# Splits moved to VectorE, early squares to ScalarE, late products over 128 rows, and a read that alternates halves

## The chip, the cores and the metric

The kernel runs on one core of one Trainium2 chip. The metric is the device time of one execution in microseconds. The kernel before was timed three times; the median is 1171.35 us (1170.88 to 1172.41).

## The reference

Three stages follow each other. Every number is float32; the weights of the second and third stage are drawn as float64, and the kernel reads their 64-bit words.

```python
# x [8, 8, 512, 64], state [8, 8, 32, 64] (batch, head, token, width), scale = 1/8
a  = softmax(scale * x @ state^T)            # token over state rows
xread = a @ state
a2 = softmax(scale * state @ x^T)            # state row over tokens
sread = a2 @ x
x = concat([xread, sread], axis=2)           # 8 * 544 = 4352 rows of 512
h = x @ w_in;  r = maximum(h, 0);  x = (r * r) @ w_out        # 512 -> 2048 -> 512
h = x @ w2_in                                                 # 512 -> 1024
solu = h * softmax(h)
out = layernorm(solu) * g_ln @ w2_out                         # 1024 -> 512
```

## The kernel before

TensorE takes operands of a rounded 32-bit type (F32R), so a number is kept as two of them: a rounded part (`hi`) and the rest (`lo`). `split` (L106) makes both: ScalarE copies into `hi` with rounding, and another engine subtracts `hi` from the source into `lo`. `triple` (L110) then makes a product from three matmuls: hi by hi (L114), hi by lo (L115), lo by hi (L116).

The read of the state is not computed token by token. For each batch of x, state and w_in are multiplied first (`sw_part` for batches 0 to 3, `late_part` for batches 4 to 7), written to DRAM, and read back by `load_sw` in chunks of 512 columns. `split_sw` (L368) splits a chunk's two tiles (`sw`), 64 splits in all, whose subtraction runs on GpSimd through the argument `eng`. `hidden` (L535) multiplies them with the attention weights `ah`, `al` of the batch into a bank of PSUM (`ps_h`, two banks), ScalarE applies Relu, and the result `r` is squared, by ScalarE in the first 16 steps (L546), by VectorE later (L548). One step later `high` (L551) rounds the square into `gh` (a cast on VectorE, L553), `low` makes the rest `gl` (VectorE, L558), and another step later `project` multiplies both with a tile of w_out into four accumulators `acc`.

A step is one column block of 128 (f) of one batch (b). The list `items` runs batches 0 and 1 in two halves (steps 0 to 31), batches 2 to 7 (steps 32 to 127), and then the rows of `sread` (b = 8, steps 128 to 143, 256 columns wide). In the first 20 steps the words of w_in and w_out are converted to 32 bits, mostly by VectorE (`convert_parts`, L182 to L199). From step 32 to 63 each second step also holds two late products (`late_part`): state tiles transposed once (`st_t`, hi and lo) by w_in tiles that hold the hi rows of one head in partitions 0 to 63 and its lo rows in partitions 64 to 127. L340 multiplies over all 128 rows, L341 the lo part of the state over the first 64.

`attention(b)` is a list of pieces that the steps before call one after the other: transposes of x (`trans_x`, L400), scores (L413, L414), softmax by row (`rows_a`, `rows_b`) and by column, transposes of the weights (`trans_a`, L507), and `sread` (L474), which multiplies x with the column weights: 32 instructions of 64 weight columns in two bursts for each batch, each recorded as two matmuls. The two heads of a pair write partitions 0 to 63 and 64 to 127 of one bank.

After the last step the third stage runs tile by tile (`up`, `solu_norm`, `trans`, `down`).

The code is not the order of the engines. A scheduler takes the instructions in the order of the program and places each on its engine by its own estimate of when it becomes ready; each engine, and the DMA queue of SyncE (SP), then runs its list strictly in order. A change in one engine's work can so move instructions of all others.

Of the kernel before, what the change touches and what calls it, by code (L numbers as in the profile page):

```python
# [8 lines left out]
F32 = mybir.dt.float32  # L9
# [3 lines left out]
AF = mybir.ActivationFunctionType  # L13
ALU = mybir.AluOpType
# [6 lines left out]
def memory_attention_relu2_solu(  # L21
# [15 lines left out]
    nc = tc.nc  # L37
    P = 128
    B, H, S, D = x.shape
# [5 lines left out]
    NT = S // P  # L45
    NHP = H // 2
    NQ = H // 4
    NF = F1 // P
# [54 lines left out]
    ]  # L103
    sr = srp.tile([P, NHP, NSR], F32, name="sr")

    def split(hi, lo, src, eng=None):  # L106
        nc.scalar.activation(out=hi, in_=src, func=AF.Copy)  # L107
        (eng or nc.vector).tensor_tensor(out=lo, in0=src, in1=hi.bitcast(F32), op=ALU.subtract)  # L108

    def triple(ps, pairs, first, last):  # L110

        n = len(pairs)
        for i, (lh, ll, rh, rl) in enumerate(pairs):
            nc.tensor.matmul(out=ps, lhsT=lh, rhs=rh, start=first and i == 0, stop=False)  # L114
            nc.tensor.matmul(out=ps, lhsT=lh, rhs=rl, start=False, stop=False)  # L115
            nc.tensor.matmul(out=ps, lhsT=ll, rhs=rh, start=False, stop=last and i == n - 1)  # L116

    def bank(name):
        return ps_m.tile([P, 512], F32, tag="m", name=name)
# [7 lines left out]
    def sw_tile(name):  # L127
        return swp.tile([P, 2, 512], F32R, tag="sw", name=name)
# [126 lines left out]
    def state_step(a, t):  # L255

        ps = bank("ps_st")
        for bb in range(2):
            for q in range(NQ):
                o = (bb * NQ + q) * P  # L260
                nc.tensor.transpose(
                    ps[:, o : o + P], a[:, 2 * t + bb, q].rearrange("p i d -> p (i d)"), ident
                )
        v = ps.rearrange("p (b q i n) -> p q n b i", b=2, q=NQ, i=2)
        for i in range(2):
            o = bd[i][t]
            split(o[:, :, i], o[:, :, 1 - i], v[:, :, :, :, i])
# [31 lines left out]
    def late_state(step):  # L299
        nb = B // 2  # L300
        if step == 0:
            t = stgp.tile([P, H, 2, D], F32, tag="stg", name="st_l")
            for b in range(nb):
                for i in range(2):
                    nc.sync.dma_start(
                        out=t[b * NS : (b + 1) * NS, :, i, :], in_=state[nb + b].rearrange("h n d -> n h d")
                    )
            late_st["f32"] = t
        else:
            t = late_st["f32"]  # L310
            ps = bank("ps_st")
            for k in range(4):
                nc.tensor.transpose(
                    ps[:, k * P : (k + 1) * P], t[:, 4 * (step - 1) + k].rearrange("p i d -> p (i d)"), ident
                )
            o = u_tile("st_t")
            split(o[:, 0, :], o[:, 1, :], ps)
            late_st[step - 1] = o
# [11 lines left out]
    def late_part(u, i):  # L330
        c, k = divmod(u, NM)
        if i == 0:
            sw_ev[0] = evp.tile([P, 2, 512], F32, tag="ev", name="ev_sw")
        ev = sw_ev[0]
        ps = bank("ps_sw")
        t = late_w[u]
        h = 2 * k + i
        st = late_st[h // 4]
        o = (h % 4) * P
        nc.tensor.matmul(out=ps, lhsT=st[:, 0, o : o + P], rhs=t[:, i, :], start=True, stop=False)  # L340
        nc.tensor.matmul(out=ps, lhsT=st[:D, 1, o : o + P], rhs=t[:D, i, :], start=False, stop=True)  # L341
        nc.scalar.activation(out=ev[:, i, :], in_=ps, func=AF.Copy)
        if i == 1:
            nc.sync.dma_start(out=sw2_d[:, 2 * k : 2 * k + 2, c * FC : (c + 1) * FC], in_=ev)
            late_w.pop(u)
# [22 lines left out]
    def split_sw(b, c):  # L368
        st = loading.pop((b, c))
        loaded[b, c] = []  # L370
        for q in range(NQ):
            t = sw_tile("sw")
            split(t[:, 0, :], t[:, 1, :], st[:, q, :], nc.gpsimd)
            loaded[b, c].append(t)

    def load_w1in(c, kk):
# [16 lines left out]
    def attention(b):  # L393
# [82 lines left out]
        def sread(half):  # L476
            if half == 0:
                v["ps_sr"] = bank("ps_sr")
            ps = v["ps_sr"]
            for hp in (2 * half, 2 * half + 1):  # L480
                for i in range(2):
                    h = 2 * hp + i
                    for t in range(NT):
                        nc.tensor.matmul(  # L484
                            out=ps[i * D : (i + 1) * D, hp * NS : (hp + 1) * NS],
                            lhsT=xs_t[b][hp][:, t, i, :],
                            rhs=v["e2", t // 2][:, t % 2, h * NS : (h + 1) * NS],
                            start=(t == 0),
                            stop=(t == NT - 1),
                        )  # L490
            if half == 1:
                nc.scalar.activation(
                    out=sr[:, :, b * NS : (b + 1) * NS],
                    in_=ps[:, : NHP * NS].rearrange("p (h n) -> p h n", n=NS),
                    func=AF.Copy,
                )
# [13 lines left out]
        def at(f, *a):  # L510
# [14 lines left out]
            [at(cols_t, 0)],  # L525
            [at(cols_t, 1)],
            [at(sread, 0)],
            [at(sread, 1)],
        ]

# [3 lines left out]
    def hidden(blk, f, w, ah, al, n):  # L534

        c0 = (f % FPC) * P
        ps = ps_h.tile([P, 512], F32, tag="h", name="ps_h")[:, :n]
        pairs = [
            (w[k][:, 0, c0 : c0 + P], w[k][:, 1, c0 : c0 + P], ah[:, k, :], al[:, k, :])
            for k in range(ah.shape[1])  # L540
        ]
        triple(ps, pairs, True, True)
        r = rp.tile([P, 512], F32, tag="r", name="r")[:, :n]
        nc.scalar.activation(out=r, in_=ps, func=AF.Relu)  # L544
        if len(done) < NF:
            nc.scalar.activation(out=r, in_=r, func=AF.Square)  # L546
        else:
            nc.vector.tensor_tensor(out=r, in0=r, in1=r, op=ALU.mult)  # L548
        return r

    def high(b, f, n, r):  # L551
        gh = gp.tile([P, 512], F32R, tag="gh", name="gh")[:, :n]
        nc.vector.tensor_copy(out=gh, in_=r)  # L553
        return b, f, n, r, gh

    def low(b, f, n, r, gh):
# [76 lines left out]
    while first:  # L633
        for piece in first.pop(0):
            piece()
    fetch_pair(NM)
    split_sw(0, 0)
    begin("o", 0)
    for t in range(1, B // 2):
# [56 lines left out]
    def up(s, blk, t):  # L696
        xh, xl, _ = x2_t[blk]
        ps = ps_2[s % 2].tile([P, F2], F32, tag="h2", name="h2")
        for k in range(NM):
            for lt, hl in ((xh, (0, 1)), (xl, (0,))):  # L700
                for i in hl:
                    for a in range(2):
                        nc.tensor.matmul(  # L703
                            out=ps[:, a * 512 : (a + 1) * 512],
                            lhsT=lt[:, k, t * P : (t + 1) * P],
                            rhs=w2[k][:, i, a * 512 : (a + 1) * 512],
                            start=(k == 0 and lt is xh and i == 0),
                            stop=(k == NM - 1 and lt is xl),
                        )
        return ps  # L710
# [78 lines left out]
    done = []  # L789
    for s, (b, f) in enumerate(items):  # L790
# [24 lines left out]
        if b == B:  # L815
# [9 lines left out]
            if f in (12, 13):  # L825
                split_x2(0)
        h = high(*squares.pop(0)) if squares else None
        if ws == 2 and 1 <= w < B - 1:
            att = attention(w + 1)
# [9 lines left out]
        if h:  # L839
            pend.append(low(*h))  # L840
        squares.append((b, f, n, hidden(b, f, loaded[b, f // FPC], *a1_t[b], n)))
        done.append((b, f))
        if s // FPC + 1 < len(chunks) and chunks[s // FPC + 1][0] < B:
            nxt = chunks[s // FPC + 1]
            if s % FPC == 1:
                load_sw(*nxt)
            elif s % FPC == 2:
                split_sw(*nxt)
        if b < 2 and f in (NF - 4, NF - 3):
            i = f - NF + 4  # L850
# [12 lines left out]
        for m in range(4):  # L863
            if s < 24 or m == 0:
                advance()
            if sw is not None and m < 2:
                sw_part(sw, m)
            if late is not None and m > 1:
                late_part(late, m - 2)
            if job:  # L870
                project(*job, m)
# [22 lines left out]
    for s in range(1, len(tiles) + 2):  # L894
        if s == 1:
            reload_w2(7, 1)
        if s < len(tiles):
            blk, t = tiles[s]
            i = order.index(blk) + 1
# [7 lines left out]
            ps = up(s, blk, t)  # L907
# [36 lines left out]
```

## Time and profile before

| | |
|---|---|
| median of three runs | 1171.35 us |
| profiled execution | 1172.12 us, span 1170.3 us |
| granted TensorE clock, mean | 0.983 |
| TensorE busy | 1124.8 us (96%) |
| VectorE busy | 746.5 us (64%) |
| ScalarE busy | 484.1 us (41%) |
| GpSimd busy | 143.9 us (12%) |
| DMA queue of SyncE | 132.68 MB, 36.5% of 16 engines |

The span is the time from the first to the last instruction that the profile shows; the profiled execution is 1.8 us longer than its span. Busy times are unions: matmuls overlap each other, and one of 0.39 us may start 0.23 us after the one before it, so the distance between starts tells what a matmul costs, and not how long it lasts. Step 0 begins at about 57 us, step 16 at 162 us, step 32 at 243 us, step 64 at 421 us, step 128 at 712 us; the third stage fills the time from 760 us on.

### The profile page before, as it was taken

What the parts mean: (1) busy time and instruction counts of PE and PEld (TensorE: products, weight loads), DVE (VectorE), ACT (ScalarE), POOL (GpSimd) and SP (SyncE); (2) the same over time, 40 slices, a digit from 0 to 9 for tenths busy, and PEclk for the clock granted to TensorE, in tenths of its full rate; (3) what the DMA queues carried; (4) which work ended last, traced back from release to release, by engine and by line L of the source; (5) the groups of instructions that cost most, each with busy time, mean ns of one, the idle gap of its engine ahead of it and who ended that gap; (6) DMA issues with size and microseconds to landing.
All of it is one profiled execution on the core that took longest, in us unless ns stands there. A gap on an engine that the chain in (4) does not pass through costs nothing.

```text
span 1170.3 us, 15242 instructions
## 1 busy us (share of the span) xinstructions
PE 1124.8 (96%) x5672; PEld 914.3 (78%) x5672; DVE 746.5 (64%) x1357; ACT 484.1 (41%) x845; POOL 143.9 (12%) x122
## 2 busy tenths in 40 slices
PE   4787999999999999999999999999999999999997
PEld 2556778777777778888888889988888888888886
DVE  7869999778557569588585554765545454445442
ACT  4657664345445345244342212443434333334232
POOL 0101302132221122222111110000000000000000
PEclk9788999999999999999999999999999999999999
DMA  8775794567565454331310114621101011000000
GB/s 228 242 231 184 267 286 127 161 184 223 180 180 176 128 165 135 89 119 64 91 37 18 73 54 150 229 82 54 64 19 63 18 63 37 28 18 27 19 26 30
DMA packets 93323, 133.66 MB, mean 114 GB/s; under 512 B 45248, under 2 KB 45760, under 8 KB 93248
## 3 DMA queue, kind: packets, MB, share of 16 engines
q1 hardware_dynamic: 93248, 132.68, 36.5%
q8 instruction: 45, 0.74, 0.3%
q14 instruction: 30, 0.25, 0.1%
HBM read 83.37 MB, written 49.28 MB: 113 GB/s over the span
## 4 chain that ended last, share of the span: by engine, by line
PE 84%; DVE 8%; DMA 3%; ACT 2%; issue 1%; POOL 1%; SPq 0%; POOLq 0%; ACTq 0%; DVEq 0%
PE h L703 15%; PE acc L114 10%; PE acc L115 9%; PE acc L116 9%; PE ps_o L754 5%; PE ps_o L752 5%; PE ps_o L753 5%; PE ps_h L114 5%; PE ps_h L116 5%; PE ps_h L115 5%; PE ps_t L742 2%; PE ps_sr L484 2%; PE ps_sw L341 1%; DMA stg<-sw_d 1%; PE ps_x L400 1%
## 5 line engine op out<-in xcount | busy, mean ns | idle before, releaser
L114 PE MATMUL acc<-gh,w1out 128*128 128x512 f32 (+1 forms) x576 | 223.5, 389 | 5.3 <-DVE gh L553 3.9
L115 PE MATMUL acc<-gl,w1out 128*128 128x512 f32 (+1 forms) x576 | 219.4, 381 | 0.0
L116 PE MATMUL acc<-gh,w1out 128*128 128x512 f32 (+1 forms) x576 | 219.2, 381 | 0.0
L548 DVE TENSOR_TENSOR r<-r 128x512 f32<-128x512 f32 (+1 forms) x128 | 99.5, 778 | 119.4 <-ACT r L544 119.3
L108 POOL TENSOR_TENSOR sw<-stg,sw 128x512 fp32r<-128x512 f32 x64 | 101.0, 1590 | 417.1 <-ACT sw L107 245.3
L703 PE MATMUL h<-w,x2h 128*128 128x512 f32 x544 | 148.6, 395 | 0.0
L544 ACT ACTIVATE r<-ps_h 128x512 f32<-128x512 f32 (+1 forms) x144 | 82.3, 572 | 134.9 <-PE ps_h L116 131.2
L114 PEld LDWEIGHTS acc<-gh,w1out 128*128 128x128 f32 x576 | 109.4, 190 | 34.1 <-issue 7.4
L116 PEld LDWEIGHTS acc<-gh,w1out 128*128 128x128 f32 x576 | 109.3, 190 | 20.7
L115 PEld LDWEIGHTS acc<-gl,w1out 128*128 128x128 f32 x576 | 109.5, 190 | 19.8 <-issue 0.5
L703 PEld LDWEIGHTS h<-w,x2h 128*128 128x128 f32 x544 | 99.7, 188 | 18.9
L114 PE MATMUL ps_h<-ah,sw 128*128 128x512 f32 x256 | 107.7, 421 | 0.9 <-ACT ah L107 0.9
L752 PE MATMUL ps_o<-w,lh 128*128 128x512 f32 x272 | 106.1, 390 | 1.0 <-ACT lh L107 1.0
L754 PE MATMUL ps_o<-w,ll 128*128 128x512 f32 x272 | 106.2, 390 | 0.6 <-DVE ll L108 0.6
L753 PE MATMUL ps_o<-w,lh 128*128 128x512 f32 x272 | 105.9, 389 | 0.0
L116 PE MATMUL ps_h<-ah,sw 128*128 128x512 f32 x256 | 101.9, 398 | 1.4 <-POOL sw L108 1.4
L558 DVE TENSOR_TENSOR gl<-r,gh 128x512 fp32r<-128x512 f32 (+1 forms) x144 | 100.5, 698 | 3.4
L115 PE MATMUL ps_h<-al,sw 128*128 128x512 f32 x256 | 101.0, 394 | 0.0
L721 ACT ACTIVATE e<-h,nm 128x1024 f32<-128x1024 f32 x34 | 38.0, 1116 | 143.7 <-DVE nm L718 143.7
L717 DVE TENSOR_REDUCE nm<-h 128x1 f32<-128x1024 f32 x34 | 41.6, 1224 | 86.1 <-PE h L703 86.1
L553 DVE CAST gh<-r 128x512 fp32r<-128x512 f32 (+1 forms) x144 | 80.6, 560 | 9.8 <-ACT r L546 1.9
L703 PE MATMUL h<-w,x2l 128*128 128x512 f32 x272 | 83.8, 389 | 0.0
(131 smaller groups left out, 1715.9 us busy)
## 6 DMA issues: line engine op xcount, KB each, us to landing
stg<-sw_d SPq DMA_DIRECT2D x128, 128.0 KB, 3.0
sw_d<-ev_sw SPq DMA_DIRECT2D x28, 512.0 KB, 4.1
st<-in_moe_w_out_dram SPq DMA_DIRECT2D x24, 512.0 KB, 4.7
xs<-in_x_dram SPq DMA_DIRECT2D x64, 128.0 KB, 3.2
w1i_d<-w1in SPq DMA_DIRECT2D x16, 512.0 KB, 3.9
st<-in_moe_w_in_dram SPq DMA_DIRECT2D x16, 512.0 KB, 5.3
x_d<-ev_x SPq DMA_DIRECT2D x16, 512.0 KB, 2.7
w1in<-w1i_d SPq DMA_DIRECT2D x32, 256.0 KB, 4.7
```

Of the source, the lines that this page charges most:

```text
L108: (eng or nc.vector).tensor_tensor(out=lo, in0=src, in1=hi.bitcast(F32), op=ALU.subtract)
L114: nc.tensor.matmul(out=ps, lhsT=lh, rhs=rh, start=first and i == 0, stop=False)
L115: nc.tensor.matmul(out=ps, lhsT=lh, rhs=rl, start=False, stop=False)
L116: nc.tensor.matmul(out=ps, lhsT=ll, rhs=rh, start=False, stop=last and i == n - 1)
L544: nc.scalar.activation(out=r, in_=ps, func=AF.Relu)
L548: nc.vector.tensor_tensor(out=r, in0=r, in1=r, op=ALU.mult)
L553: nc.vector.tensor_copy(out=gh, in_=r)
L558: nc.vector.tensor_tensor(out=gl, in0=r, in1=gh.bitcast(F32), op=ALU.subtract)
L703: nc.tensor.matmul(out=ps[:, a * 512 : (a + 1) * 512], lhsT=lt[:, k, t * P : (t + 1) * P], rhs=w2[k][:, i, a * 512 : (a + 1) * 512], start ...
L752: nc.tensor.matmul(out=ps, lhsT=a, rhs=wt[:, 0, o : o + 512], start=(k == 0), stop=False)
L753: nc.tensor.matmul(out=ps, lhsT=a, rhs=wt[:, 1, o : o + 512], start=False, stop=False)
L754: nc.tensor.matmul(out=ps, lhsT=bb, rhs=wt[:, 0, o : o + 512], start=False, stop=(k == NK - 1))
```

## The change

Four edits. (1) `split_sw` no longer names GpSimd: its 64 subtractions go to VectorE, and `split` loses the argument. (2) For steps 0 to 31 (b < 2) ScalarE makes both the rounded square and the square, from `r`, in `high`; VectorE neither squares nor casts there. From step 32 on VectorE still squares, as `r` times the product in PSUM, and casts. (3) L341 multiplies over 128 rows, so that the lo part of the state also meets the lo part of w_in. (4) `sread` runs over the four token blocks outside and the two heads inside, so that its matmuls alternate between the two halves of the partitions.

```diff
-    def split(hi, lo, src, eng=None):
+    def split(hi, lo, src):
         nc.scalar.activation(out=hi, in_=src, func=AF.Copy)
-        (eng or nc.vector).tensor_tensor(out=lo, in0=src, in1=hi.bitcast(F32), op=ALU.subtract)
+        nc.vector.tensor_tensor(out=lo, in0=src, in1=hi.bitcast(F32), op=ALU.subtract)
...
         nc.tensor.matmul(out=ps, lhsT=st[:, 0, o : o + P], rhs=t[:, i, :], start=True, stop=False)
-        nc.tensor.matmul(out=ps, lhsT=st[:D, 1, o : o + P], rhs=t[:D, i, :], start=False, stop=True)
+        nc.tensor.matmul(out=ps, lhsT=st[:, 1, o : o + P], rhs=t[:, i, :], start=False, stop=True)
...
-            split(t[:, 0, :], t[:, 1, :], st[:, q, :], nc.gpsimd)
+            split(t[:, 0, :], t[:, 1, :], st[:, q, :])
...
             for hp in (2 * half, 2 * half + 1):
-                for i in range(2):
-                    h = 2 * hp + i
-                    for t in range(NT):
+                for t in range(NT):
+                    for i in range(2):
+                        h = 2 * hp + i
...
         nc.scalar.activation(out=r, in_=ps, func=AF.Relu)
-        if len(done) < NF:
-            nc.scalar.activation(out=r, in_=r, func=AF.Square)
-        else:
-            nc.vector.tensor_tensor(out=r, in0=r, in1=r, op=ALU.mult)
+        if len(done) >= 2 * NF:
+            nc.vector.tensor_tensor(out=r, in0=r, in1=ps, op=ALU.mult)
         return r
 
     def high(b, f, n, r):
         gh = gp.tile([P, 512], F32R, tag="gh", name="gh")[:, :n]
-        nc.vector.tensor_copy(out=gh, in_=r)
+        if b < 2:
+            nc.scalar.activation(out=gh, in_=r, func=AF.Square)
+            nc.scalar.activation(out=r, in_=r, func=AF.Square)
+        else:
+            nc.vector.tensor_copy(out=gh, in_=r)
         return b, f, n, r, gh
```

The scheduler's lists change in the first 32 steps above all. Three places follow, each before and after. Numbers behind a name tell tiles of one name apart.

SP's queue ahead of step 0 to 2, before (`st64` are words of w_in or w_out, `xs` a head of x for attention 1, `sw_d` and `w1i_d` go out to DRAM):

```order
L289 DMA sw_d0_57<-ev_sw_522 256x1x512
L213 DMA w1i_d2_64<-w1in_534 256x1x512
L289 DMA sw_d1_58<-ev_sw_581 256x1x512
L213 DMA w1i_d3_65<-w1in_593 256x1x512
L289 DMA sw_d2_59<-ev_sw_606 256x1x512
L390 DMA xs_630<-in_x_dram 128x4x64
L289 DMA sw_d3_60<-ev_sw_618 256x1x512
L390 DMA xs_633<-in_x_dram 128x4x64 x2
L390 DMA xs_636<-in_x_dram 128x4x64 x2
L390 DMA xs_639<-in_x_dram 128x4x64 x2
L137 DMA st64_645<-in_moe_w_in_dram 128x1024
L137 DMA st64_647<-in_moe_w_out_dram 128x1024
```

and after:

```order
L137 DMA st64_643<-in_moe_w_out_dram 128x1024
L287 DMA sw_d2_59<-ev_sw_475 128x512
L287 DMA sw_d3_60<-ev_sw_485 128x512
L213 DMA w1i_d0_62<-w1in_463 256x1x512
L137 DMA st64_645<-in_moe_w_in_dram 128x1024
L213 DMA w1i_d1_63<-w1in_492 256x1x512
L289 DMA sw_d0_57<-ev_sw_522 256x1x512
L213 DMA w1i_d2_64<-w1in_534 256x1x512
L289 DMA sw_d1_58<-ev_sw_581 256x1x512
L213 DMA w1i_d3_65<-w1in_593 256x1x512
L289 DMA sw_d2_59<-ev_sw_606 256x1x512
L390 DMA xs_630<-in_x_dram 128x4x64 x2
```

The load `st64_645`, tile 8 of w_in (counted from 0), moved from behind all loads of x to a place ahead of the first, behind the first `w1i_d` of its group.

VectorE's list in steps 0 to 3 up to the second score of attention 1 (`xl` and `st` belong to attention 1), before:

```order
L199 SCALAR_TENSOR_TENSOR w1out_407<-cu_686,cz_683 128x512
L188 SCALAR_TENSOR_TENSOR cu_751<-st64_643,cu_751 128x512
L553 CAST gh_773<-r_740 128x512
L558 TENSOR_TENSOR gl_790<-r_740,gh_773 128x512
L553 CAST gh_841<-r_799 128x512
L558 TENSOR_TENSOR gl_863<-r_799,gh_841 128x512
L553 CAST gh_924<-r_872 128x512
L558 TENSOR_TENSOR gl_955<-r_872,gh_924 128x512
L108 TENSOR_TENSOR xl_655<-ps_x_649,xh_654 128x512
L419 TENSOR_TENSOR st_658<-ps_s_659,st_658 64x512
L108 TENSOR_TENSOR xl_670<-ps_x_664,xh_669 128x512
L419 TENSOR_TENSOR st_658<-ps_s_702,st_658 64x512
```

and after:

```order
L192 SCALAR_TENSOR_TENSOR ch_759<-st64_643,cz_747 128x512
L188 SCALAR_TENSOR_TENSOR cu_756<-st64_645,cu_756 128x512
L192 SCALAR_TENSOR_TENSOR ch_762<-st64_645,cz_753 128x512
L198 TENSOR_SCALAR cz_747<-ch_759 128x512
L198 TENSOR_SCALAR cz_753<-ch_762 128x512
L199 SCALAR_TENSOR_TENSOR w1out_697<-cu_750,cz_747 128x512
L199 SCALAR_TENSOR_TENSOR w1in_698<-cu_756,cz_753 128x512
L560 TENSOR_TENSOR gl_790<-r_740,gh_772 128x512
L560 TENSOR_TENSOR gl_863<-r_799,gh_840 128x512
L108 TENSOR_TENSOR xl_655<-ps_x_649,xh_654 128x512
L560 TENSOR_TENSOR gl_955<-r_872,gh_923 128x512
L419 TENSOR_TENSOR st_658<-ps_s_659,st_658 64x512
```

The casts are gone, and the conversions of two tiles (`st64_643`, w_out for step 2, and `st64_645`) now stand ahead of attention 1; before, they stand behind its third `xl`.

TensorE's list in attention 1, before, from the first transposes of x to the last score (`ps_x`, `ps_s`), and the first product of step 2 (`gh_841`):

```order
L400 MATMUL ps_x_664<-ident_142,xs_633 128x128 x4
L413 MATMUL ps_s_702<-xh_669,bd1_0_150 128x512
L414 MATMUL ps_s_702<-xl_670,bd1_0_150 128x512
L400 MATMUL ps_x_707<-ident_142,xs_636 128x128 x4
L413 MATMUL ps_s_717<-xh_712,bd0_0_146 128x512
L414 MATMUL ps_s_717<-xl_713,bd0_0_146 128x512
L400 MATMUL ps_x_722<-ident_142,xs_639 128x128 x4
L413 MATMUL ps_s_775<-xh_727,bd1_0_150 128x512
L414 MATMUL ps_s_775<-xl_728,bd1_0_150 128x512
L425 MATMUL ps_r_780<-ident_142,st_658 128x128
L114 MATMUL acc0_814<-gh_841,w1out_698 128x512
L115 MATMUL acc0_814<-gl_863,w1out_698 128x512
```

and after, where `gh_840` is step 2's:

```order
L114 MATMUL acc0_813<-gh_840,w1out_697 128x512
L115 MATMUL acc0_813<-gl_863,w1out_697 128x512
L116 MATMUL acc0_813<-gh_840,w1out_697 128x512
L413 MATMUL ps_s_702<-xh_669,bd1_0_150 128x512
L114 MATMUL acc1_814<-gh_840,w1out_697 128x512
L115 MATMUL acc1_814<-gl_863,w1out_697 128x512
L414 MATMUL ps_s_702<-xl_670,bd1_0_150 128x512
L400 MATMUL ps_x_707<-ident_142,xs_636 128x128 x4
L116 MATMUL acc1_814<-gh_840,w1out_697 128x512
L114 MATMUL acc2_815<-gh_840,w1out_697 128x512
L115 MATMUL acc2_815<-gl_863,w1out_697 128x512
L116 MATMUL acc2_815<-gh_840,w1out_697 128x512
```

Step 2's products now stand between the scores of attention 1; before, they stand behind the last of them.

## Rows read from the trace of the kernel before

**Rows 1.** Busy time of each engine by stretch; first the columns.
```profile
core 0: us, PE busy (x) PEld busy (x) DVE busy (x) ACT busy (x) POOL busy (x), PEclk, DMA share, GB/s
57.00:162.00 105.00, 92.65 (x432) 71.10 (x433) 91.45 (x179) 68.27 (x124) 18.22 (x8) 0.92 0.73 241
162.00:242.70 80.70, 77.55 (x413) 63.05 (x412) 68.84 (x117) 35.59 (x65) 18.16 (x12) 1.00 0.61 163
242.70:420.60 177.90, 177.90 (x865) 133.32 (x864) 114.09 (x191) 79.68 (x139) 34.19 (x23) 1.00 0.59 177
420.60:496.30 75.70, 75.37 (x402) 62.01 (x401) 58.38 (x100) 31.46 (x56) 16.98 (x12) 1.00 0.42 127
```

**Rows 2.** Timeline of TensorE about one late product: start, us, engine, line.
```profile
302.75 0.39 PE L116 MATMUL acc<-gh,w1out 128*128 128x512 f32 x1
302.97 0.39 PE L340 MATMUL ps_sw<-w1in,st_t 128*128 128x512 f32 x1
303.29 0.50 PE L341 MATMUL ps_sw<-w1in,st_t 64*128 64x512 f32 x1
303.72 0.50 PE L114 MATMUL acc<-gh,w1out 128*128 128x512 f32 x1
304.06 0.39 PE L115 MATMUL acc<-gl,w1out 128*128 128x512 f32 x1
```

**Rows 3.** The line L341: count, duration in ns (min/median/max), first and last start.
```profile
L341 PE MATMUL ps_sw<-w1in,st_t x32: 492/498/499, 248.2 to 416.4; 64*128 64x512 f32 x32
```

**Rows 4.** Timeline of TensorE: a burst of the state's read and what follows.
```profile
321.05 1.43 PE L484 MATMUL ps_sr<-e,xs 128*64 128x32 f32 x32
322.41 0.50 PE L114 MATMUL ps_h<-ah,sw 128*128 128x512 f32 x1
```

**Rows 5.** The line L484, as in rows 3.
```profile
L484 PE MATMUL ps_sr<-e,xs x512: 222/223/244, 53.2 to 644.8; 128*64 128x32 f32 x171
```

**Rows 6.** Busy time of L484 alone in two stretches of that burst.
```profile
321.00:321.26 0.26, 0.21 (x4) 0.21 (x4) 1.00 1.07 229
321.52:321.78 0.26, 0.26 (x16) 0.26 (x12) 1.00 0.13 24
```

**Rows 7.** Groups by form: line, operation, count | busy us, mean ns | idle before.
```profile
L108 POOL TENSOR_TENSOR sw<-stg,sw 128x512 fp32r<-128x512 f32 x64 | 101.0, 1590 | 417.1 <-ACT sw L107 245.3 <-PE ps_h L116 82.9 <-DMA stg<-sw_d 58.3
L548 DVE TENSOR_TENSOR r<-r 128x512 f32<-128x512 f32 x112 | 92.8, 829 | 108.7 <-ACT r L544 108.6
L553 DVE CAST gh<-r 128x512 fp32r<-128x512 f32 x128 | 75.9, 593 | 8.7 <-ACT r L546 1.9 <-PE acc L116 1.1
L108 DVE TENSOR_TENSOR al<-ps_a,ah 128x512 fp32r<-128x512 f32 x16 | 11.0, 686 | 10.6 <-ACT ah L107 10.6
L546 ACT ACTIVATE r<-r 128x512 f32<-128x512 f32 x16 | 10.1, 630 | 0.1
```

**Rows 8.** The lines L548 and L553, as in rows 3.
```profile
L548 DVE TENSOR_TENSOR r<-r x128: 417/691/1789, 164.0 to 758.4; 128x512 f32<-128x512 f32 x112, 128x256 f32<-128x256 f32 x16
L553 DVE CAST gh<-r x144: 293/427/1552, 59.7 to 758.9; 128x512 fp32r<-128x512 f32 x128, 128x256 fp32r<-128x256 f32 x16
```

**Rows 9.** Timeline of SP's DMA issues before step 2's weights.
```profile
66.70 5.17 SPq L390 DMA_DIRECT2D xs<-in_x_dram  x6
71.92 0.62 SPq L137 DMA_DIRECT2D st<-in_moe_w_in_dram  x1
```

**Rows 10.** Timeline of VectorE in attention 1; in brackets idle time and what ended it.
```profile
77.05 0.43 DVE L182 TENSOR_SCALAR cz<-st 128x512 uint32<-128x512 uint32 x1 [0.20 <-DMA st<-in_moe_w_in_dram]
86.74 0.69 DVE L435 TENSOR_REDUCE mx<-ps_r 128x16 f32<-128x512 f32 x1 [2.22 <-PE ps_r L425]
```

**Rows 11.** Timeline of TensorE behind attention 1's scores.
```profile
81.50 0.79 PE L114 MATMUL acc<-gh,w1out 128*128 128x512 f32 x1 [1.12 <-ACT w1out L195]
86.21 0.93 PE L425 MATMUL ps_r<-ident,st 128*128 128x128 f32 x7
103.96 0.77 PE L114 MATMUL acc<-gh,w1out 128*128 128x512 f32 x1 [3.95 <-DVE gh L553]
```

## The prediction

> **What bounds the kernel now.** I read the busy time by stretch first [rows 1]. From 242.70 to 420.60 us (steps 32 to 63) TensorE is busy for all 177.90 us at full clock, and from 420.60 to 496.30 (steps 64 to 79) for 75.37 of 75.70. VectorE has 114.09 and 58.38 us of work there. So from step 32 on the time is TensorE's own: a cycle that TensorE no longer spends is a cycle off the end, and one saved on VectorE is worth nothing. Before that it is otherwise. In steps 0 to 15 (57 to 162 us) VectorE works 91.45 of 105 us, TensorE 92.65 at a mean granted clock of 0.92, and in steps 16 to 31 TensorE idles 80.70 - 77.55 = 3.15 us. There TensorE waits for others, and the order in which VectorE works decides.
>
> Then the order of time on TensorE inside the full stretch, to see what its cycles go to. A product over 128 rows and 512 columns starts 0.22 to 0.23 us after the one before it (302.75 to 302.97). The late product over 64 rows breaks this [rows 2]: it starts 0.32 us after L340, the next one 0.43 us after it, and the one after that another 0.34 us later. 302.97 to 304.06 is 1.09 us for three starts that take 0.68 elsewhere.
>
> Last, the front: what TensorE waits for between 69 and 104 us [rows 9 to 11].
>
> **The change part by part.**
>
> *Late products over 128 rows.* Each L341 costs 1.09 - 0.68 = 0.41 us beyond an ordinary product. It is no longer work: the 64-row product streams the same 512 columns, and lasts longer (498 ns) than a full one (0.39). There are 32 [rows 3], all in the stretch without idle time: 32 x 0.41 = 13.1 us. The stage confirms the size: steps 32 to 63 take 5.56 us each (177.90/32), steps 64 to 79 take 75.70/16 = 4.73, and the 0.83 between them is one late pair a step, which would be 2 x 0.23 at the ordinary rate: 0.37 too much, x 32 = 12 us. Over 128 rows L341 has the shape of L340, which costs the ordinary step wherever no L341 stands beside it. Bounds: 0 (if something else than the row count breaks the rhythm) to 13.1. I take 13.0. What is late next: VectorE, at 114 us of work in then 165, still has room.
>
> *The state's read.* A burst is 32 records in 1.43 us [rows 4], some 1.21 from first start to last start, since a record lasts 0.22 [rows 5]. In its first 0.21 us four records run, some 60 ns each. In its middle 16 records touch a window of 0.26 us [rows 6]; with 0.22 us each that is 16/0.48, one per 30 ns: there a second half's records run beside the first's. Alternating halves should give that rate from the start: 32 x 0.03 = 0.96, so 0.25 us less a burst. There are 512/32 = 16 bursts, four of them in the front where TensorE waits anyway; 12 x 0.25 = 3.0 us. Bounds: 3.0 gained, or, if every alternation is served at the first window's rate, 32 x 0.06 = 1.92, 0.71 lost a burst and 8.5 in all. I take 3.0, because the middle of the burst is the very case of two halves in flight.
>
> The Trainium skill says otherwise in one place: "TensorE: Matmul & The Clock Gate", Part 3, has weight loads overlap running products only where the row groups differ, and the two halves here differ in columns alone. By that rule alternating gains nothing, and the sum is 3 us higher. The middle of the burst, at twice the rate of its head with the rows unchanged, speaks against it. "TensorEngine Tiling (Array Packing)", Key Properties, lets different tiles load and multiply in parallel, which is what the trace shows.
>
> *Splits from GpSimd to VectorE.* 64 instructions of 1590 ns leave GpSimd [rows 7]. On VectorE a subtract of that size takes 686 ns (al, with an operand in PSUM): 64 x 0.69 = 44 us more. But GpSimd's work slows VectorE today: the square L548 takes 691 ns in the median and 1789 at most, the cast L553 427 and 1552 [rows 8], and their means are 829 and 593 [rows 7]. That is 112 x 0.138 + 128 x 0.166 = 36.7 us on these two lines alone. So VectorE's load from step 32 on stays about where it is, 64 to 77% of the stretch [rows 1], and hides the splits. Without that cover each would cost at most its 0.69.
>
> *Square and rounded part on ScalarE for steps 0 to 31.* VectorE loses 16 casts (0.43 each) in steps 0 to 15 and 16 casts and 16 squares in steps 16 to 31: 6.9 us and 16 x (0.43 + 0.69) = 17.9 us. ScalarE gains 16 and 32 squares of 630 ns [rows 7], 10 and 20 us, beside 68.27 of 105 and 35.59 of 80.70 now: it has the room. In exchange come at most 8 splits (5.5 us) and 12 (8.3 us), as many as GpSimd ran in these stretches [rows 1]. VectorE net: 1.4 us and 9.6 us less, more with the slowing gone.
>
> *What the new order does to the front.* SP issues tile 8 of w_in (st64_645, counted from 0) at 71.92, behind eight loads of x whose last six take 5.17 us [rows 9]. VectorE meets its words at 77.05 and waits for them [rows 10], and the conversion of step 2's w_out stands behind that. So the first of step 2's twelve products starts at 81.50, after a wait for w1out, and they take 4.7 us, part of it at half clock, before the scores' transposes at 86.21 [rows 11]. VectorE has waited 2.22 us for them at 86.74. After the change SP issues that tile 12 places earlier, VectorE converts both tiles ahead of attention 1, and TensorE has step 2's products between the links of the score chain, where it idles today. The 4.7 us block leaves the path. At 103.96 TensorE has waited 3.95 us for a cast on VectorE; that cast is ScalarE's now, and the gl behind it comes as early as VectorE's queue lets it. I add the 1.4 us of VectorE above and 1 us of slowing: 7.1 us for steps 0 to 15. Of the 3.15 us of idle time in steps 16 to 31, I take 2. Before step 0 two splits join a full VectorE queue, 2 x 0.69 at most, and end 0.9 us sooner each than on GpSimd: 0.7 lost, give or take. Bounds for the front together: 2 us lost (the splits, nothing gained) to 24 gained (12.35 us of idle time, 8% of 105 us of clock, and the 3.15).
>
> *The multiply that reads PSUM (step 32 on).* Same engine, same duration (686 against 691 ns). But a bank of ps_h is now free after VectorE's multiply, not after ScalarE's Relu. There are two banks: from the end of a layer's product to the next use of its bank pass two steps less two products, 2 x 4.73 - 2 x 6 x 0.23 = 6.7 us; Relu and multiply need 1.3. I count nothing; the third rival below says what happens if VectorE is over 5 us late.
>
> **Sum:** 13.0 + 3.0 + 7.1 + 2.0 - 0.7 = 24.4 us. The profiled execution took 1172.12 us, 0.77 above the median of the runs, so 1171.35 - 24.4 = 1147 us.
>
> **Rivals.**
>
> *Only TensorE's cycles come off.* Attention 1 still begins when its x lands, and VectorE, with the splits in its queue, is as late after it as today. For it: VectorE works 91 of 105 us. Against it: the block at 81.50 waits for an order, not for work. 1171.35 - 13.0 - 3.0 + 0.7 = 1156.
>
> *The front gives more.* If steps 0 to 15 end without idle time and at full clock, up to 24 us instead of 9: halfway there the time is 1139. Against it: the transfers, at 0.73 of their engines already [rows 1].
>
> *VectorE holds the banks: slower than before.* In steps 32 to 143 splits, w2 conversions and attention come in clusters; if VectorE runs over 5 us behind the Relu, TensorE waits for a bank at L114 each time. It decides from 24.4/112 = 0.22 us a step on; at 0.3 us a step the time is 1147 + 34 = 1181. For it: VectorE is at 77% in steps 64 to 79. Against it: the slowing by GpSimd goes as the splits come.
>
> *Alternating halves is served one by one.* 8.5 us lost instead of 3.0 gained: 1158.5. The case of the page's rule in its harder form.
>
> **How the numbers follow.** My forecast 0.56 (its own range 1141 to 1152), TensorE's cycles alone 0.22, more from the front 0.12, halves one by one 0.06, banks 0.04. 1138 to 1157 leaves out the upper part of the second and fourth, the far end of the third and the banks, under 0.2 together. About 0.2% (2.3 us) is what a measurement of this kernel can tell from no change. Only the banks, or several losses at once, reach it: faster 0.95, same 0.01, slower 0.04.
>
> **What would show it.** In the profile after: L340, L341 and their neighbours all at 0.23 us, and steps 32 to 63 some 165 us long; bursts of L484 under 1.0 us from first to last start; no GpSimd work beside VectorE before step 32, and L553's median as its mean; step 2's products between 69 and 81 us. I am wrong if the 64-row rhythm persists with 128 rows, if L114 into ps_h waits for VectorE, or if the stretch before step 32 is no shorter.

## The result, and the profile after

The changed kernel takes 1143.28 us (median of four runs, 1141.79 to 1144.04) against 1171.88 for the kernel before on the same chip: a ratio of 0.9755, 95% interval 0.9738 to 0.9772, 28.6 us less. The forecast was 1147, with a range from 1138 to 1157.

The profiled execution took 1141.79 us, the fastest of the four. The stretches of [rows 1] (steps 0 to 15, 16 to 31, 32 to 63, 64 to 79), with the columns of that group:

```profile
48.10:152.20 104.10, 94.73 (x512) 73.25 (x512) 92.47 (x189) 82.08 (x149) 0.00 (x0) 0.95 0.79 259
152.20:228.50 76.30, 76.22 (x411) 62.47 (x410) 51.46 (x94) 54.18 (x97) 2.58 (x2) 1.00 0.62 172
228.50:392.50 164.00, 164.00 (x865) 134.49 (x865) 110.27 (x207) 79.72 (x138) 9.40 (x7) 1.00 0.65 192
392.50:467.10 74.60, 74.60 (x401) 61.42 (x401) 55.73 (x108) 31.54 (x56) 5.18 (x4) 1.00 0.42 131
```

Steps 32 to 63 fell from 177.90 to 164.00 us, steps 64 to 79 from 75.70 to 74.60. Step 32 begins at 228.5 instead of 242.7. Steps 16 to 31 hold almost no idle time of TensorE any more (76.22 us busy of 76.30, before 77.55 of 80.70). In the whole stretch from 228.5 to 700 us the trace lists no wait of TensorE. From step 80 on the two kernels differ by 1.0 us.

TensorE about a late product, as in [rows 2]:

```profile
294.19 0.39 PE L116 MATMUL acc<-gh,w1out 128*128 128x512 f32 x1
294.42 0.39 PE L340 MATMUL ps_sw<-w1in,st_t 128*128 128x512 f32 x1
294.64 0.39 PE L341 MATMUL ps_sw<-w1in,st_t 128*128 128x512 f32 x1
294.87 0.39 PE L114 MATMUL acc<-gh,w1out 128*128 128x512 f32 x1
295.10 0.39 PE L115 MATMUL acc<-gl,w1out 128*128 128x512 f32 x1
```

Every start is 0.22 to 0.23 us behind the one before; the 0.32, 0.43 and 0.34 of [rows 2] are gone. A burst of the state's read, as in [rows 4]:

```profile
301.34 1.12 PE L484 MATMUL ps_sr<-e,xs 128*64 128x32 f32 x32
302.40 0.50 PE L114 MATMUL ps_h<-ah,sw 128*128 128x512 f32 x1
```

1.12 us instead of 1.43. With the last record's 0.22 taken off, the first and last start lie 0.90 us apart instead of 1.21.

SP's issues about tile 8 of w_in (its load is the second row), to be held against [rows 9]:

```profile
47.94 0.56 SPq L213 DMA_DIRECT2D w1i_d<-w1in  x1
48.54 1.39 SPq L137 DMA_DIRECT2D st<-in_moe_w_in_dram  x1
...
64.68 5.51 SPq L390 DMA_DIRECT2D xs<-in_x_dram  x6
```

It is issued at 48.54 us, no longer at 71.92. TensorE in attention 1, where [rows 11] have the block at 81.50:

```profile
70.74 0.63 PE L400 MATMUL ps_x<-ident,xs 128*128 128x128 f32 x4 [1.68 <-DMA xs<-in_x_dram]
71.12 0.48 PE L116 MATMUL acc<-gh,w1out 128*128 128x512 f32 x1
71.44 0.39 PE L114 MATMUL acc<-gh,w1out 128*128 128x512 f32 x1
71.67 0.40 PE L115 MATMUL acc<-gl,w1out 128*128 128x512 f32 x1
71.90 0.40 PE L116 MATMUL acc<-gh,w1out 128*128 128x512 f32 x1
72.14 0.43 PE L413 MATMUL ps_s<-xh,bd 128*128 128x512 f32 x1
```

The `acc` products fill the places between the links of the score chain. VectorE's lines, as in [rows 7]:

```profile
L546 DVE TENSOR_TENSOR r<-r,ps_h 128x512 f32<-128x512 f32 x96 | 65.8, 685 | 90.5 <-ACT r L544 90.3
L108 DVE TENSOR_TENSOR sw<-stg,sw 128x512 fp32r<-128x512 f32 x64 | 45.2, 708 | 22.9 <-ACT sw L107 22.2 <-DMA xs<-in_x_dram 0.5
L555 DVE CAST gh<-r 128x512 fp32r<-128x512 f32 x96 | 40.7, 424 | 4.2
```

The square's mean fell from 829 to 685 ns, the cast's from 593 to 424. The 64 splits cost VectorE 45.2 us, where the prediction had 44.

The longest wait of TensorE ahead of step 32 is for one `gl` (engine and line, what it waited for, us in total, times, longest):

```profile
PE acc L115 <- DVE gl L560: 2.9, 1, 2.9
```

It stands at 97.52 us, shortly ahead of step 6, as the 3.95 us wait for a cast does in the kernel before [rows 11].

### The profile page after: what moved, and what is told of

The parts are those of the page before. It is cut to its first block, busy times and chain, and to the rows that moved or that the text cites. A ratio compares the mean times of both kernels' runs of the same rounds, so it can differ in the third digit from the quotient of the medians.

```text
span 1140.1 us, 15182 instructions
## 1 busy us (share of the span) xinstructions
PE 1099.8 (96%) x5672; PEld 908.3 (80%) x5672; DVE 712.0 (62%) x1373; ACT 511.0 (45%) x893; POOL 40.8 (4%) x58
## 4 chain that ended last, share of the span: by engine, by line
PE 89%; ACT 4%; DVE 3%; DMA 3%; issue 1%; SPq 0%; POOLq 0%; POOL 0%; ACTq 0%
PE h L705 16%; PE acc L114 10%; PE acc L116 10%; PE acc L115 10%; PE ps_h L114 6%; PE ps_h L116 5%; PE ps_h L115 5%; PE ps_o L756 5%; PE ps_o L754 5%; PE ps_o L755 5%; PE ps_t L744 2%; PE ps_sr L484 1%; PE ps_x L400 1%; DMA st<-in_moe_w_out_dram 1%; PE ps_sw L340 1%
## 5 line engine op out<-in xcount | busy, mean ns | idle before, releaser
L114 PE MATMUL acc<-gh,w1out 128*128 128x512 f32 (+1 forms) x576 | 218.5, 381 | 2.8 <-ACT w1out L195 1.8
L116 PE MATMUL acc<-gh,w1out 128*128 128x512 f32 (+1 forms) x576 | 218.9, 380 | 0.0
L546 DVE TENSOR_TENSOR r<-r,ps_h 128x512 f32<-128x512 f32 (+1 forms) x112 | 72.4, 647 | 102.1 <-ACT r L544 101.9
L560 DVE TENSOR_TENSOR gl<-r,gh 128x512 fp32r<-128x512 f32 (+1 forms) x144 | 95.6, 665 | 11.9 <-ACT r L553 8.9
L731 ACT ACTIVATE j<-e,mu 128x1024 f32<-128x1024 f32 x34 | 39.1, 1151 | 54.6 <-DVE mu L728 50.6
L756 PEld LDWEIGHTS ps_o<-w,ll 128*128 128x128 f32 x272 | 51.1, 188 | 12.0 <-DVE ll L108 1.5
```

The costliest lines, as they stand in the source:

```text
L546: nc.vector.tensor_tensor(out=r, in0=r, in1=ps, op=ALU.mult)
L560: nc.vector.tensor_tensor(out=gl, in0=r, in1=gh.bitcast(F32), op=ALU.subtract)
L731: nc.scalar.activation(out=j, in_=e, func=AF.Square, bias=mu, accum_out=var)
L756: nc.tensor.matmul(out=ps, lhsT=bb, rhs=wt[:, 0, o : o + 512], start=False, stop=(k == NK - 1))
```

## The experiments

Each was timed beside the kernel before on one chip; that kernel's medians there were 1172.04, 1171.65 and 1171.55 us. The changed kernel's 1143.28 us, with which some of them are compared, is that of the section above. A reader of the profiles has to know how far two executions of one list drift apart. The three rows below are of the changed kernel, of the kernel with L341 over 64 rows, and of the one with GpSimd's splits from batch 2 on, all for 20 to 60 us (columns as in [rows 1]):

```profile
20.00:60.00 40.00, 28.87 (x173) 20.13 (x173) 35.99 (x81) 28.56 (x57) 0.00 (x0) 0.87 0.78 259
```
```profile
20.00:60.00 40.00, 29.64 (x169) 21.86 (x170) 34.14 (x77) 26.81 (x53) 0.00 (x0) 0.79 0.75 245
```
```profile
20.00:60.00 40.00, 29.72 (x166) 21.85 (x166) 33.42 (x75) 26.37 (x52) 0.00 (x0) 0.72 0.72 238
```

Their lists are the same there, yet TensorE's mean granted clock was 0.87, 0.79 and 0.72, and step 0 began at 48.1, 49.6 and 51.2 us. So for the front (everything ahead of step 32) a difference of 3 us between two profiles proves nothing, and medians decide. By its own profile the changed kernel gained 14.2 us ahead of step 32; by the medians it is 28.6 less the 16.0 that lie behind step 32, 12.6. (Of these, 0.6 belong to edit 4: two of its bursts lie just ahead of step 32.)

**Edit 3 alone, and undone.**

```diff
# on the kernel before
+        nc.tensor.matmul(out=ps, lhsT=st[:, 1, o : o + P], rhs=t[:, i, :], start=False, stop=True)
# on the changed kernel
+        nc.tensor.matmul(out=ps, lhsT=st[:D, 1, o : o + P], rhs=t[:D, i, :], start=False, stop=True)
```

Alone: 

> The kernel before with edit 3 alone (L341 over 128 rows); every engine's list of instructions is that of before. Row count breaks the rhythm: L340, L341 and the products behind them start 0.23 us apart, steps 32 to 63 shrink from 177.9 to about 165 us, the total falls by 13 us to 1158.5 (1157.5 to 1160). Rival, the late pair costs this much for another reason (its bank, its tile of w_in, the ScalarE copy behind it): 1171.5, with the starts still 0.32 and 0.43 us apart.

Measured 1159.73 us, ratio 0.9893 (0.9873 to 0.9912), 12.3 less. Undone: 

> The changed kernel with edit 3 undone (L341 over 64 rows again; the lists of all engines are those of the changed kernel). If edit 3's gain stands by itself whatever the rest does: 1143.3 + 12.3 = 1155.6, steps 32 to 63 back from 164.0 to 176 us. If it needs the earlier squares or splits: under 1150.

Measured 1156.53 us, ratio 0.9882 (0.9865 to 0.9899): 13.25 more than the changed kernel. L341 in the two kernels, alone and undone (columns as in [rows 3]):

```profile
L341 PE MATMUL ps_sw<-w1in,st_t x32: 389/389/395, 247.7 to 404.1; 128*128 128x512 f32 x32
```
```profile
L341 PE MATMUL ps_sw<-w1in,st_t x32: 493/498/498, 235.0 to 402.3; 64*128 64x512 f32 x32
```

No list moves in either, so the row count by itself sets the 498 ns and, as the times show, the cost. Steps 32 to 63 took 165.7 us alone and 176.7 undone.

**Edit 4 alone.** The diff is that of the change to `sread`.

> The kernel before with edit 4 alone (sread alternates halves). Two halves in flight: a burst's first-to-last start falls from 1.21 to 0.90 us; 12 bursts behind step 32 give 12 x 0.31 = 3.7 us, the four in the front 0 to 1.2: 1167.2 (1166 to 1168.5). Rival, the shorter bursts of the changed kernel come from something else in it: bursts stay at 1.2 us and the time at 1171.5.

Measured 1169.98 us, ratio 0.997 (0.9955 to 0.9986), nine runs from 1165.2 to 1171.3: 2.1 less, and above the range that was expected. TensorE in its trace:

```profile
322.67 1.13 PE L484 MATMUL ps_sr<-e,xs 128*64 128x32 f32 x32
323.72 0.50 PE L114 MATMUL ps_h<-ah,sw 128*128 128x512 f32 x1
```

The burst is short by the order alone. Behind step 32, where ten of the twelve bursts lie, its profile is 3.1 us shorter than that of before (1.2 in steps 32 to 63, 1.9 in steps 64 to 127). 1.6 us went back to the front, where the runs scatter.

**Edit 1 alone, edit 2 alone.**

```diff
# edit 1 on the kernel before
-            split(t[:, 0, :], t[:, 1, :], st[:, q, :], nc.gpsimd)
+            split(t[:, 0, :], t[:, 1, :], st[:, q, :])
```

> The kernel before with edit 1 alone (all 64 splits on VectorE). Theory A, the order makes the front's gain: this edit alone moves the load of w_in tile 8 ahead of the x loads and spreads step 2's twelve products over attention 1, so steps 0 to 15 end some 8 to 10 us sooner and the rest is unchanged (32 to 63 still 177.9): 1162 (1160 to 1165). Theory B, relief of VectorE by the squares and casts made the gain: here VectorE only gets 44 us more work and no relief, so 1171 to 1175. Theory C, GpSimd no longer slows VectorE: the gain is spread over steps 0 to 31 in proportion to the splits there (20 of 64), 2 to 5 us: 1168.

Measured 1164.32 us, ratio 0.9926 (0.9909 to 0.9943): 7.7 less.

> The kernel before with edit 2 alone (ScalarE squares and rounds up to step 32). Its lists keep the load of w_in tile 8 behind the x loads and step 2's twelve products in one block ahead of attention 1's transposes. Theory A (order): only steps 16 to 31 gain, 2 to 4 us, steps 0 to 15 about 1: 1168 (1166.5 to 1170). Theory B (relief of VectorE): most of the front's 14 us comes here, 1160 to 1163. Theory C (GpSimd's slowing): 1170 to 1171.5.

Measured 1169.59 us, ratio 0.9978 (0.9963 to 0.9993): 2.5 less. The relief of VectorE (theory B) falls: the edit that loads VectorE with 44 us more brought three times as much as the one that unloads it. But the 7.7 us of edit 1 are not all in steps 0 to 15: 3.1 of them are in steps 16 to 31 (77.7 us instead of 80.8), so theory A alone doesn't hold either.

**Edit 2 undone.** 

> The changed kernel with edit 2 undone (VectorE squares and rounds in the first 32 steps as before). The three other edits by themselves then: 1143.3 + 2.5 = 1146 if edit 2's gain is the same with and without the splits; up to 1149 if VectorE, which has the splits now, needs the relief.

Measured 1146.36 us, ratio 0.9786 (0.9771 to 0.9801): 3.1 more than the changed kernel, the same as edit 2 alone within the runs' scatter.

**Which part of edit 1: two splits, or the other 62.** In each of the three runs `split` has its argument `eng` back.

```diff
# the first chunk's two back on GpSimd
+            split(t[:, 0, :], t[:, 1, :], st[:, q, :], nc.gpsimd if (b, c) == (0, 0) else None)
# all but these
+            split(t[:, 0, :], t[:, 1, :], st[:, q, :], None if (b, c) == (0, 0) else nc.gpsimd)
# those of batches 2 to 7
+            split(t[:, 0, :], t[:, 1, :], st[:, q, :], nc.gpsimd if b >= 2 else None)
```

Two: 

> The changed kernel with two of the 64 splits, those of the first chunk, back on GpSimd. That alone brings back the old list around attention 1: w_in tile 8 behind the x loads, step 2's twelve products in one block ahead of the transposes. Theory A (the order makes most of the front's gain): 5 to 9 us lost before step 8, 1148 to 1152. Theory C (GpSimd slows VectorE): two splits are nothing, 1143 to 1145.

Measured 1148.70 us, ratio 0.9811 (0.979 to 0.9832): 5.4 lost by two instructions out of 64. TensorE in its trace:

```profile
80.94 0.79 PE L114 MATMUL acc<-gh,w1out 128*128 128x512 f32 x1 [1.12 <-ACT w1out L195]
...
85.80 1.01 PE L425 MATMUL ps_r<-ident,st 128*128 128x128 f32 x7
```

That is the block of [rows 11] again, with the same wait of 1.12 us ahead of it. The two splits themselves begin at 34.8 and 48.4 us, and the trace lists no wait of TensorE's matmuls for them (one weight load waits 0.8 us): the order costs the time. It costs it there. Summed over its matmuls, TensorE has started 64,000 columns by 71.1 us in this trace and 80,000 by 90.4 us. In the changed kernel's it is 71.1 and 84.3 us, in the two other traces of its lists (the rows above) 72.0 and 83.9, 74.4 and 87.7.

Sixty-two: 

> The changed kernel with 62 of the 64 splits back on GpSimd; only those of the first chunk stay on VectorE, and with them the new list around attention 1. Theory A: the gain of steps 0 to 11 stays, and what splits beside VectorE cost in steps 12 to 31 is lost, 1 to 4 us: 1144.5 to 1147.5. Theory C: nearly all of the 7 us that edit 1 gained in the front alone is lost, 1149 to 1151.

Measured 1149.05 us, ratio 0.9813 (0.9798 to 0.9827): 5.8 lost, more than theory A allowed, with the new order around attention 1 kept (the lists of TensorE, VectorE and ScalarE are the changed kernel's up to 83 us and differ behind). The two splits bore theory A out, but it doesn't hold alone: the time lies in theory C's range, and GpSimd costs time too. The longest waits of TensorE in its trace between 98 and 120 us, and the two GpSimd instructions behind the first of them:

```profile
PE ps_h L116 <- POOL sw L108: 2.8, 2, 2.1
PE acc L115 <- DVE gl L560: 2.0, 1, 2.0
```
```profile
108.08 7.35 POOL L108 TENSOR_TENSOR sw<-stg,sw 128x512 fp32r<-128x512 f32 x2 [21.70 <-DVE cu L187]
```

Two splits take 7.35 us where the mean of one is 1.42 in that kernel. TensorE waits for them itself: up to step 32 it waits 4.4 us for splits of GpSimd, in four places. The wait for `gl` is no loss of this run: the changed kernel has it with 2.9 us.

Forty-eight: 

> The changed kernel with the 48 splits of batches 2 to 7 back on GpSimd; the first 32 steps' lists hardly change. The prediction's claim that the splits are neutral where TensorE sets the time: 1143 to 1144.5, with squares and casts of VectorE slowed again. Rival, VectorE's relief there is worth time (a bank freed late, a late sread): 1146 or more.

Measured 1142.37 us, ratio 0.9759 (0.9744 to 0.9773), the changed kernel's time. From step 32 on it makes no difference where the splits run.

**Does GpSimd cost by slowing VectorE, or by being late?**

```diff
+            if b < 2 and (b, c) != (0, 0):
+                junk = rp.tile([P, 512], F32, tag="junk", name="junk", bufs=1)
+                nc.gpsimd.tensor_tensor(out=junk, in0=st[:, q, :], in1=st[:, q, :], op=ALU.subtract)
```

> The changed kernel, splits on VectorE as there, with 14 idle subtractions on GpSimd at the places of the splits of steps 3 to 31 (same size, read from the same staging tile, result read by nobody); the lists of TensorE are those of the changed kernel. Theory S (GpSimd beside VectorE slows VectorE, and so TensorE): most of what the run with 62 splits on GpSimd lost comes back as a loss, 1147 to 1149. Theory L (a split on GpSimd is itself late, and TensorE waits for it; nobody waits for these): 1143 to 1145.

Measured 1147.90 us, ratio 0.9787 (0.9772 to 0.9802): 4.6 lost to 14 instructions that nobody waits for, with the lists of TensorE, VectorE and ScalarE unchanged: theory S costs time by itself. The size is uncertain, as the five runs lie between 1144.7 and 1148.8. Nor is it theory S's share in the run with 62 splits: there TensorE's waits are for GpSimd itself (theory L), here for VectorE. GpSimd and VectorE about 130 us (line numbers behind L373 are three higher in this kernel):

```profile
129.16 3.07 POOL L376 TENSOR_TENSOR junk<-stg 128x512 f32<-128x512 f32 x2 [16.23 <-DMA stg<-sw_d]
```
```profile
129.21 0.67 DVE L563 TENSOR_TENSOR gl<-r,gh 128x512 fp32r<-128x512 f32 x1
129.81 1.52 DVE L108 TENSOR_TENSOR sw<-stg,sw 128x512 fp32r<-128x512 f32 x1
131.25 1.26 DVE L198 TENSOR_SCALAR cz<-ch 128x512 uint32<-128x512 uint32 x1
132.44 0.41 DVE L187 TENSOR_SCALAR cu<-st 128x512 uint32<-128x512 uint32 x1
132.77 0.68 DVE L199 SCALAR_TENSOR_TENSOR w1in<-cu,cz 128x512 fp32r<-128x512 f32 x1
133.37 0.68 DVE L108 TENSOR_TENSOR sw<-stg,sw 128x512 fp32r<-128x512 f32 x1
```

and TensorE:

```profile
134.10 0.50 PE L116 MATMUL ps_h<-ah,sw 128*128 128x512 f32 x1 [1.29 <-DVE sw L108]
```

The split takes 1.52 instead of 0.68 us and the L198 behind it 1.26 instead of 0.41: 1.7 us of VectorE, of which 1.29 arrive at TensorE as a wait for the second split. The same happens about 153 us, where two conversions take 1.5 us each and TensorE waits 0.92 and 0.60 us for the splits behind them. These three waits, 2.8 us, are what this trace shows of the 4.6; where the rest is lost stays open.

**Towards a faster version.**

```diff
# project: the product by gl last (both runs)
+        nc.tensor.matmul(out=a, lhsT=hi, rhs=gh, start=f % part == 0, stop=False)
+        nc.tensor.matmul(out=a, lhsT=lo, rhs=gh, start=False, stop=False)
+        nc.tensor.matmul(out=a, lhsT=hi, rhs=gl, start=False, stop=f % part == part - 1)
# attention: both halves of sread in one piece (second run only)
-            [at(sread, 0)],
-            [at(sread, 1)],
+            [at(sread, 0), at(sread, 1)],
```

> The changed kernel with the product by gl as the last of each three in project. TensorE waits 2.9 us for one gl in the first 32 steps; with two products ahead of it instead of one, and the list moved with it: 1140 to 1143. Rival, that wait is covered by another right behind it: 1143.3.

Measured 1143.40 us, ratio 0.9759 (0.9746 to 0.9772). The wait for `gl` fell from 2.9 to 2.0 us, and the time stayed: the rival was right.

> As the run before, and both halves of sread in one piece, so that a burst has 64 instead of 32 instructions: a burst's exit (0.15 us) and entry are saved once for each batch behind step 32, some 6 x 0.3 = 2 us: 1138 to 1141. Rival, the longer burst only moves the wait of a product behind it: as the run before.

Measured 1140.24 us, ratio 0.974 (0.9722 to 0.9759). The burst of 64:

```profile
301.18 2.06 PE L484 MATMUL ps_sr<-e,xs 128*64 128x32 f32 x64
303.17 0.50 PE L114 MATMUL ps_h<-ah,sw 128*128 128x512 f32 x1
```

From its first start to the next product's start 1.99 us pass, where two bursts of 32 records (16 instructions) take 2 x 1.06; and a burst's entry is paid once instead of twice: it starts 0.32 us behind the product before it, in both kernels, where two products are 0.23 apart. By its profile steps 32 to 127 are 1.4 us shorter than the changed kernel's. It is 3.2 us faster than the run before on the same chip, and by the median the fastest of all; the intervals overlap, so it may be less.

## Why the prediction was right, and where it was small

**Late products: right.** 13.0 forecast; 12.3 alone, 13.25 undone, and 12.2 or 12.7 in the stage itself. The remainder had been worked out from three starts in one place, and the stage's own time had given 12: the truth lies between the two. That L340 keeps the ordinary step where no L341 stands beside it was no reading of the trace, as behind each of its 32 stands an L341; the changed kernel's rows show the step at last.

**The state's read: right in mechanism, 0.06 us too small per burst.** 0.25 was forecast and 0.31 came, 3.7 us for the 12 bursts from 220 us on. Six of them lie in steps 64 to 127, which are 1.9 us shorter with edit 4 alone (6 x 0.31) and 2.4 in the changed kernel (291.4 to 289.0). The rival of halves served one by one is out. The Trainium skill, "TensorE: Matmul & The Clock Gate", Part 3, has weight loads overlap running products only where the row groups differ. The prediction had worked out from it that alternating gains nothing, and the measurement decides against that: these halves differ in columns alone, and their bursts became shorter by a quarter.

**Splits neutral from step 32 on: right,** shown by the 48 put back. It holds although GpSimd slows VectorE there as before. The cast L555 in that kernel, and in the changed one:

```profile
L555 DVE CAST gh<-r x112: 293/427/1555, 232.3 to 731.2; 128x512 fp32r<-128x512 f32 x96, 128x256 fp32r<-128x256 f32 x16
```
```profile
L555 DVE CAST gh<-r x112: 293/422/429, 229.9 to 729.0; 128x512 fp32r<-128x512 f32 x96, 128x256 fp32r<-128x256 f32 x16
```

With TensorE busy throughout, VectorE's 1555 ns are paid from its own slack. The rival in which VectorE holds the banks of ps_h is out: TensorE has no wait from 228.5 to 700 us in the changed kernel.

**Step 2's block: right in place; what was measured is the order as a whole.** 4.7 us were forecast for the block, and 5.4 come back with the old order, which two splits decide. They are lost where the block stands, between 71 and 90 us by the count of columns above. How much of them is the block, and how much the lower clock there (81 to 87 us: 0.59, in the changed kernel 0.83), no run separates. The prediction had described the new order but not said which edit makes it.

**Squares and casts on ScalarE: right in direction.** Edit 2 gives 2.5 us alone and 3.1 undone. The forecast's 1.4 us for steps 0 to 15 were tied to it. The 2.0 for the idle time of steps 16 to 31 were tied to no edit, and were too small: that stretch, from its first Relu to that of step 32, fell by 4.5 us (80.8 to 76.3), 0.6 of it by two bursts, and either edit alone brings most of it (77.7 us with edit 1, 77.8 with edit 2). TensorE's wait of 3.95 us for a cast, for which the prediction counted nothing, became the 2.9 us for `gl`.

**GpSimd's slowing in the front: the step that failed, by its size.** The prediction put 1 us on it for steps 0 to 15 and otherwise set the splits off against the squares and casts by VectorE's busy time. In the changed kernel, GpSimd work that nobody waits for costs 4.6 us by the medians, and 62 splits on GpSimd cost 5.8. In the kernel before it may have been less: of the 7.7 us of edit 1 alone, 5.4 for the order leave 2.3. Two readings were at fault. It took the means (+138 and +166 ns) as load, and a load is right only where VectorE has slack. In the front, where VectorE works 91 of 105 us, one collision was 1.7 us, and 1.29 of it arrived at TensorE. And it took GpSimd's own mean of 1590 ns for its duration everywhere. The kernel before shows otherwise (GpSimd, then VectorE):

```profile
113.92 7.52 POOL L108 TENSOR_TENSOR sw<-stg,sw 128x512 fp32r<-128x512 f32 x2 [22.08 <-DMA stg<-sw_d]
```
```profile
117.58 0.42 DVE L553 CAST gh<-r 128x512 fp32r<-128x512 f32 x1
117.92 0.68 DVE L188 SCALAR_TENSOR_TENSOR cu<-st,cu 128x512 f32<-128x512 uint32 x1
119.22 1.09 DVE L192 SCALAR_TENSOR_TENSOR ch<-st,cz 128x512 uint32<-128x512 uint32 x1 [0.61 <-ACT cz L183]
120.23 1.76 DVE L558 TENSOR_TENSOR gl<-r,gh 128x512 fp32r<-128x512 f32 x1
```

Up to 118.6 us VectorE runs back to back at its ordinary times (0.42, 0.68), and the first of GpSimd's two splits lasts from 113.92 to 119.76; behind VectorE's pause of 0.61 us GpSimd gets through, and then VectorE is the slow one. This row was there to be read.

**Start: -0.7 forecast, and no loss found.** Step 0's Relu begins between 47.9 and 52.1 us wherever the first two splits run on VectorE, and between 56.2 and 57.2 in the five kernels where they run on GpSimd (before, and edits 2, 3 and 4 alone among them). Its products stand earlier in the new list. That lead is not a gain by itself: by the count of columns above, the kernels with the new list are no further at 71 us than the one with the old.

The front came to 12.6 us by the medians, where 8.4 was forecast (7.1 + 2.0 - 0.7). That is the whole of the difference between 24.4 forecast and 28.6 measured: behind step 32 the forecast's 13.0 + 3.0 met the 16.0 us, in part by luck, as the late products came out a little smaller and the bursts a little larger. The four edits alone add up to 7.7 + 2.5 + 12.3 + 2.1 = 24.6 us and together bring 28.6 (26.7 to 30.7 by the interval). Whether the 4 us between are an effect of the edits on each other or the scatter of edit 4's runs stays open. The two parts of edit 1, each undone in the changed kernel, lose 5.4 and 5.8, together 11.2 where edit 1 alone gave 7.7; that points to an effect of the edits on each other, but no run undoes the whole of edit 1.

## What to carry to other kernels

Before a helper engine's work is called neutral, look at its longest record and not its mean, and ask stage by stage whether the engine that it slows has slack: the same splits cost nothing from step 32 on and some 5 us before it. Where a scheduler makes the lists, find out which single instruction turns the order: here two splits of 64 decided 5.4 of the front's 12.6 us. Here a matmul over 64 rows among full ones was no saving but cost 0.38 us more (12.3 us for 32): try filling the rows if the operands allow it.

## What the runs showed of the hardware

GpSimd beside VectorE doesn't slow every VectorE instruction. The new square, whose one operand lies in PSUM, in the kernel with 48 splits on GpSimd:

```profile
L546 DVE TENSOR_TENSOR r<-r,ps_h x112: 414/687/691, 231.5 to 730.7; 128x512 f32<-128x512 f32 x96, 128x256 f32<-128x256 f32 x16
```

By start and end times 24 of the 96 wide ones overlap a GpSimd instruction, and none is longer than 691 ns. In the kernel before, the old square with both operands in SBUF averaged 1214 ns in its 30 overlaps, up to 1789 [rows 8]. The cast, with one, averaged 1300 ns in 22 overlaps in the kernel with 48 splits on GpSimd; neither is over 695 ns elsewhere. The Trainium skill, "SBUF — State Buffer", Who interferes with whom, says which instructions to expect: one of VectorE with two inputs in SBUF, or one in a two-port mode, which a cast can enter, contends with a GpSimd instruction that reads SBUF, while one with a single SBUF input outside such a mode doesn't. The runs agree on which are slowed. The half of edit 2 behind step 32 makes the square immune, and there, too, it was worth nothing (steps 32 to 63 take 177.8 us with edit 2 alone, 177.9 before), because TensorE sets the time.
